# A planned kernel's sort keys and buffer numbers replaced: attention feeding a two-layer MLP, on one core

## The chip, the core and the metric

The kernel runs on one core of one Trainium2 chip. The metric is device time in microseconds (us) of one execution; lower is better. The engines of the core that matter here are TensorE (PE; its weight loads have rows of their own, PEld), VectorE (DVE), ScalarE (ACT), GpSimd (POOL, here only a queue that issues DMAs) and SyncE (SP, a queue that issues DMAs).

## What is computed

An attention over channels (2 batches, 6016 positions, 256 channels) gives 12032 tokens of 256 values, and these go through an MLP of 2048 hidden values with a slope of its own for each negative hidden value.

```python
qn = q / (norm(q, axis=1) + 1e-6);  kn = k / (norm(k, axis=1) + 1e-6)
s = kn.transpose(0, 2, 1) @ qn / tau          # 256 x 256 for each batch
a = softmax(s)
x = (v @ a).reshape(12032, 256)
h = x @ w_in                                  # 12032 x 2048
g = maximum(h, 0) + alpha * minimum(h, 0)
out = g @ w_out                               # 12032 x 256
```

## The kernel before

**Start.** The first 91 us read q and k of both batches, form the scores, fold the softmax into w_in (one matrix M for each batch) and convert the weights. This part is written out by hand and the change doesn't touch it.

**The planned part.** From then on the kernel works through 24 tiles of 500 or 504 tokens, and in each through 8 items, each of which makes 256 hidden values: 192 items, numbered i. Every product is made of three matmuls of fp32r halves (high by high, high by low, low by high; `passes`, L723), which is why matmuls come in threes on L725, L726 and L727. Three such matmuls are called one PE step below. Each item uses a fast scheme with seven products in place of eight:

- `pe(i, p)`, p = 0 to 6, L1227: one product each, into one half of one of two PSUM tiles: `a` (from the ring `ps_q`) or `b` (from `ps_r`). Each of the two tiles fills one PSUM bank and has two halves, `[:, 0]` and `[:, 1]`; each ring has two banks. pe6 writes a's half 1; pe0, pe5, pe4 and pe3 write or add to a's half 0; pe1 adds to b's half 0 and pe2 to b's half 1.
- `copy(i, 0)` on ACT, L1244 (called copy0): copies a's half 0 to b's half 0. `copy(i, 1)` on ACT, L1247 (copy1): copies a's half 1 to an SBUF tile `p7`, in the rows `p`.
- `add(i, 0)` and `add(i, 1)` on DVE, L1251 (add0, add1): a's half 0 plus `p7`, into b's half 1 (add0) or a's half 1 (add1).
- `act_n` on ACT and `dve_g` on DVE read the whole finished bank and make g.
- Then g is split into high and low halves. Most items (128) use a second fast scheme: `g_sums`, `x_high`, `x_low`, `t_high`, `t_low` and seven products `s2` into four PSUM banks X. The other 64 use `g_high`, `g_low` and four products `out_pe` with 500 columns. `t_low` is an ACT instruction of about 1 us and a DMA on POOL's queue that adds to its result.
- At a tile's end `combine_copy`, `combine` and `finish_out` empty the X banks and send the tile out. Parallel to all this v is loaded (POOL's queue) and split for the next tile (`v_sums`, `v_high`, `v_low`), and batch 1's norms and M are prepared (`load_T`, `square_T`, `m1_pe` and others).

**What an item's chain needs.** pe0, then copy0, then pe1 and pe5; pe6, then copy1; pe5 and copy1, then add0, then pe2 and pe4; pe4, then add1, then pe3; pe2 before act_n of b, pe3 before act_n of a; dve_g of a frees the bank of `a` for pe6 of item i+2.

**What sets the order.** `put` (L1598) gives each of the 5716 steps a sort key, the running sum of the numbers that the table `AT` (L45) holds under the step's name, in hundredths of a microsecond, and the list is sorted by key (L1731). Each engine and queue executes its own instructions in the order of this list; waits between engines are set by the framework from what each instruction reads and writes. The keys are no times of the chip. The table `SLOTS` (L564) names, for each tile that is taken from a ring (`Ring`, L625), the buffer that it gets.

Of the kernel before, what the change touches and what calls it, by code (L numbers as in the profile page):

```python
# [57 lines left out]
    ),  # L58
# [12 lines left out]
    ),  # L71
# [12 lines left out]
    ),  # L84
# [12 lines left out]
    ),  # L97
    "bcast1": (44517,),
    "combine0": (
        19167, 4002, 4060, 4010, 3823, 4201, 3733, 8365, 3789, 13160, 4381, 3982, 3733, 3733, 4181,  # L100
        4058, 4000, 4046, 3834, 2959
    ),
    "combine1": (
        19506, 3766, 4010, 4063, 3883, 4037, 3941, 8242, 4046, 12990, 4435, 3805, 3923, 3720, 4162,
        4121, 3844, 3996, 3813, 3019
    ),
    "combine2": (
        19797, 3714, 4032, 4075, 4158, 3627, 4217, 7952, 4169, 13197, 3982, 4189, 3799, 4160, 4192,
        3519, 3912, 4173, 3622, 2906
    ),  # L110
    "combine_copy": (
        18933, 4158, 3999, 3670, 4206, 4128, 3843, 7850, 4122, 13259, 4085, 4338, 3202, 4316, 4109,
        4010, 3886, 4258, 3215, 3318
    ),
    "conv_a": (9754, 698, 533),
    "conv_b": (9928, 452, 433, 267),
# [12 lines left out]
    ),  # L129
# [1635 lines left out]
```

## Time and profile before

| | us |
|---|---|
| median of 3 runs | 1172.31 (1170.83 to 1172.7) |
| profiled execution: its own time | 1170.25 |
| profiled execution: span from first to last instruction | 1168.5 |

| engine | busy us | share of the span | instructions |
|---|---|---|---|
| PE (matmuls) | 1123.1 | 96% | 8076 |
| PEld (weight loads) | 1042.6 | 89% | 8076 |
| DVE | 1002.6 | 86% | 1940 |
| ACT | 890.8 | 76% | 1578 |
| POOL | 176.2 | 15% | 214 |

The end of a matmul is modelled in this profile and matmuls overlap, so PE counts as busy for a while after the last one has been issued. The time by which a weight load was held is in the rows of PEld.

### The profile page before, as it was taken

The numbers are of one execution on the slowest core, as the hardware profiler recorded it, in microseconds if no ns is written. First come the engines' busy times: TensorE is split into PE (matmuls) and PEld (weight loads), VectorE is DVE, ScalarE is ACT, GpSimd is POOL, SyncE is SP. The second block draws the span as 40 slices with busy tenths as digits, with TensorE's granted clock in tenths as the row PEclk, the third lists the DMA queues.
The fourth block names the chain that finished last, engine by engine and source line by source line (L and its number), as shares of the span: only waits on it lengthen the run. The fifth ranks groups of instructions, "written<-read, shape, count | busy, mean of one in ns | idle before, by whom it ended". The sixth has DMA issues, their size and how long they took to land.

```text
span 1168.5 us, 21606 instructions
## 1 busy us (share of the span) xinstructions
PE 1123.1 (96%) x8076; PEld 1042.6 (89%) x8076; DVE 1002.6 (86%) x1940; ACT 890.8 (76%) x1578; POOL 176.2 (15%) x214
## 2 busy tenths in 40 slices
PE   9999999999989999999999999999999999999998
PEld 8888889988988898888989889899998999989998
DVE  6798999988887888888878988798998888888886
ACT  6786787878877787677766768688887778878785
POOL 0000011111111111011100011221222212221210
PEclk9999999999999999999999999999999999999999
DMA  9996244765664655143532126556667647756644
GB/s 340 358 330 231 73 112 112 168 150 124 147 158 101 155 122 121 36 95 81 128 88 54 54 68 128 127 114 134 145 133 141 129 98 141 155 129 124 130 91 88
DMA packets 70327, 158.20 MB, mean 135 GB/s; under 512 B 6800, under 2 KB 32496, under 8 KB 70096
## 3 DMA queue, kind: packets, MB, share of 16 engines
q0 software_dynamic: 38688, 93.92, 40.2%
q1 hardware_dynamic: 31536, 62.92, 15.5%
q8 instruction: 63, 1.03, 0.4%
q14 instruction: 40, 0.33, 0.1%
HBM read 59.78 MB, written 14.42 MB: 63 GB/s over the span
## 4 chain that ended last, share of the span: by engine, by line
PE 81%; ACT 8%; DVE 7%; issue 3%; DMA 1%; SPq 0%; ACTq 0%; DVEq 0%
PE X L725 11%; PE X L726 11%; PE X L727 11%; PE a L725 11%; PE a L727 8%; PE a L726 8%; PE S L1024 7%; PE b L725 4%; PE b L727 3%; PE b L726 3%; ACT g L1263 2%; DVE g L1271 2%; DVE b L1251 1%; PE pm L1176 1%; ACT p L1247 1%
## 5 line engine op out<-in xcount | busy, mean ns | idle before, releaser
L725 PE MATMUL a<-vs,m 128*128 128x250 f32 (+1 forms) x960 | 288.7, 301 | 32.9 <-ACT p L1247 10.4
L727 PE MATMUL a<-vs,m 128*128 128x250 f32 (+1 forms) x960 | 268.9, 280 | 0.0
L726 PE MATMUL a<-vs,m 128*128 128x250 f32 (+1 forms) x960 | 268.8, 280 | 0.0
L725 PEld LDWEIGHTS a<-vs,m 128*128 128x128 f32 x960 | 181.1, 189 | 69.4 <-ACT p L1247 18.9
L1370 POOL DMA_DIRECT2D tgl<-t x128 | 111.0, 867 | 665.9 <-ACT tgl L1369 452.3
L726 PEld LDWEIGHTS a<-vs,m 128*128 128x128 f32 x960 | 182.0, 190 | 2.9
L727 PEld LDWEIGHTS a<-vs,m 128*128 128x128 f32 x960 | 182.3, 190 | 0.0
L1271 DVE SCALAR_TENSOR_TENSOR g<-g,slope,a 128x500 f32<-128x500 f32 (+1 forms) x192 | 140.4, 731 | 25.7 <-ACT g L1263 24.4
L1263 ACT ACTIVATE g<-a 128x500 f32<-128x500 f32 (+1 forms) x192 | 113.5, 591 | 59.1 <-PE a L727 50.3
L1369 ACT ACTIVATE tgl<-t 128x1000 fp32r<-128x1000 f32 (+1 forms) x128 | 133.9, 1046 | 15.1 <-DVE t L1349 8.6
L1271 DVE SCALAR_TENSOR_TENSOR g<-g,slope,b 128x500 f32<-128x500 f32 (+1 forms) x192 | 139.9, 730 | 6.2 <-ACT g L1263 5.5
L1251 DVE TENSOR_TENSOR b<-a,p 128x250 f32<-128x250 f32 (+1 forms) x192 | 81.4, 424 | 66.4 <-PE b L727 27.5
L1376 ACT CAST tgh<-t 128x1000 fp32r<-128x1000 f32 (+1 forms) x128 | 131.7, 1032 | 0.2 <-DVE t L1349 0.2
L1263 ACT ACTIVATE g<-b 128x500 f32<-128x500 f32 (+1 forms) x192 | 113.2, 590 | 20.4 <-PE b L727 16.7
L1359 DVE TENSOR_TENSOR xl<-g,xh 128x750 fp32r<-128x750 f32 (+1 forms) x128 | 119.6, 934 | 6.2 <-ACT xh L1354 6.0
L1247 ACT COPY p<-a 128x250 f32<-128x250 f32 (+1 forms) x192 | 70.8, 369 | 63.5 <-PE a L727 63.0
L725 PE MATMUL b<-vs,m 128*128 128x250 f32 (+1 forms) x384 | 110.6, 288 | 4.8 <-DVE b L1251 4.6
L1354 ACT CAST xh<-g 128x750 fp32r<-128x750 f32 (+1 forms) x128 | 105.3, 823 | 12.1 <-PE X L726 8.9
L725 PE MATMUL X<-tgh,ws 128*128 128x250 f32 (+1 forms) x384 | 107.5, 280 | 1.7 <-ACT c L1427 1.5
L1349 DVE TENSOR_TENSOR t<-g,t 128x250 f32<-128x250 f32 (+1 forms) x256 | 105.9, 414 | 2.9
L726 PE MATMUL b<-vs,m 128*128 128x250 f32 (+1 forms) x384 | 107.5, 280 | 0.0
L727 PE MATMUL b<-vs,m 128*128 128x250 f32 (+1 forms) x384 | 107.5, 280 | 0.0
(140 smaller groups left out, 2990.7 us busy)
## 6 DMA issues: line engine op xcount, KB each, us to landing
tgl<-t POOLq DMA_DIRECT2D x91, 500.0 KB, 4.5
tgl<-t POOLq DMA_DIRECT2D x37, 504.0 KB, 4.6
kqT<-kqT_dram SPq DMA_DIRECT2D x20, 512.0 KB, 4.2
kq<-k_dram SPq DMA_DIRECT2D x39, 256.0 KB, 5.6
kq<-q_dram SPq DMA_DIRECT2D x39, 256.0 KB, 5.6
v<-vT_dram POOLq DMA_DIRECT2D x16, 500.0 KB, 5.0
vs<-vt POOLq DMA_DIRECT2D x32, 250.0 KB, 4.9
outT_dram<-c SPq DMA_DIRECT2D x30, 250.0 KB, 2.8
```

The costliest lines, as they stand in the source:

```text
L725: nc.tensor.matmul(out, wh, xh, start=first, stop=False, **s)
L726: nc.tensor.matmul(out, wh, xl, start=False, stop=False, **s)
L727: nc.tensor.matmul(out, wl, xh, start=False, stop=last, **s)
L1251: nc.vector.tensor_tensor(out=h_t[i][n][:, 1, :h], in0=h_t[i][1][:, 0, :h], in1=p7_t[i][:, :h], op=ALU.add)
L1263: nc.scalar.activation(blocks(g_t[i], i, 2 * fi, 2 * fi + 2), h_t[i][fi][:, :, : half_of(i)], AF.Relu, scale=-1.0)
L1271: nc.vector.scalar_tensor_tensor(out=g, in0=g, scalar=slope[:, f : f + 1], in1=h_t[i][fi][:, :, : half_of(i)], op0=ALU.mult, op1=ALU.add,)
L1349: nc.vector.tensor_tensor(out=o, in0=x, in1=y, op=ALU.subtract)
L1354: nc.scalar.copy(xs_t[i][0][:, h : 4 * h], g_t[i][:, h : 4 * h])
L1359: nc.vector.tensor_tensor(out=xs_t[i][1][:, h : 4 * h], in0=g_t[i][:, h : 4 * h], in1=f32(xs_t[i][0][:, h : 4 * h]), op=ALU.subtract,)
L1369: nc.scalar.activation(ts[1][:, :w], tt_t[i][:, :w], AF.Copy, scale=-1.0)
L1370: nc.gpsimd.dma_start(out=ts[1][:, :w], in_=tt_t[i][:, :w], accum_op=ALU.add)
L1376: nc.scalar.copy(ts[0][:, :w], tt_t[i][:, :w])
```

## The change

Only numbers change. All keys in `AT` are new, and of `SLOTS` the strings of the rings gh, gl, raw and rn (the rings of `a`, `b`, p7 and the split v keep theirs). The set of steps, every instruction, all shapes and all DMAs stay as they are. The keys are said to come from a search that counts each wait on a PSUM tile for the whole bank.

```diff
@@ AT @@
     "act_n0": (
-        10450, 710, 501, 334, 661, 243, 586, 115, 962, 805, 144, 626, 104, 640, 689, 528, 191, 563, 575,
+        10382, 200, 905, 673, 346, 421, 345, 940, 314, 523, 497, 686, 191, 622, 415, 841, 3, 559, 825,
...
-    "keep_wi": (9983,),
-    "load_T0": (11798, 4093, 4192, 4281, 3916, 4079, 4425, 3156),
+    "keep_wi": (13308,),
+    "load_T0": (12995, 3046, 4590, 3855, 4320, 4223, 3444, 3708),
...
@@ SLOTS @@
     gh=(
-        "012012012012120120120120120121021021012012012102120102102012012012012102102102102102102102"
+        "012012012012012012012012012010210120210210210120120120120120120121201021021020120120120121"
...
```

What this makes of the order can be counted in the two sorted lists, with no run. "PE work between" is the work that the list puts on PE between the end of one step and the start of the other, taking 0.35 us for a step of three matmuls with 250 columns and 0.69 us for one with 500; under 0.9 us means two such steps or fewer.

| in the sorted list | before | after |
|---|---|---|
| items whose copy1 stands ahead of pe0 | 27 | 7 |
| of these, under 0.9 us of PE work between pe6 and pe0 | 16 | 0 |
| items whose add0 stands ahead of pe1, with under 0.9 us between pe5 and pe1 | 14 | 0 |
| items whose pe1 stands ahead of add0 | 61 | 36 |
| of these, under 0.9 us between pe1 and the first of pe2 and pe4 | 24 | 1 |
| under 0.9 us between pe0 and pe5 | 28 | 2 |
| under 0.9 us between pe5 and pe4 | 21 | 0 |
| under 0.9 us between pe4 and pe3 | 41 | 0 |
| under 0.9 us between pe5 and pe2 | 5 | 0 |
| under 0.9 us between pe0 and pe1 | 3 | 1 |
| under 1.9 us between pe3 of item i and pe6 of item i+2 | 22 | 30 |
| t_low with under 2 us between the last product that reads its buffer and itself | 46 | 71 |
| copy0 and copy1 with under 2 us between the last reader of their buffer and themselves | 88 | 118 |
| tiles whose first use of v has a key less than 10 us behind the step that frees v's buffer | 0 | 7 |

`keep_wi`, a DMA on SP's queue, stood ahead of the first `load_T` there and stands behind it now.

## Rows read from the trace of the kernel before

**Rows 1.** The page: span, busy time of engines, chain that ended last by engine.

```profile
span 1168.5 us, 21606 instructions
...
PE 1123.1 (96%) x8076; PEld 1042.6 (89%) x8076; DVE 1002.6 (86%) x1940; ACT 890.8 (76%) x1578; POOL 176.2 (15%) x214
...
PE 81%; ACT 8%; DVE 7%; issue 3%; DMA 1%; SPq 0%; ACTq 0%; DVEq 0%
```

**Rows 2.** Groups by line, PEld: busy us, mean ns, then idle before, releasers.

```profile
L727 PEld LDWEIGHTS a<-vs,m 128*128 128x128 f32 x960 | 182.3, 190 | 0.0
...
L725 PEld LDWEIGHTS a<-vs,m 128*128 128x128 f32 x960 | 181.1, 189 | 69.4 <-ACT p L1247 18.9 <-DVE b L1251 16.2 <-ACT b L1244 10.2
...
L725 PEld LDWEIGHTS b<-vs,m 128*128 128x128 f32 x384 | 72.7, 189 | 11.3 <-DVE b L1251 8.4 <-ACT b L1244 0.4
```

**Rows 3.** Waits of PEld: who waited for whom, us, times, longest.

```profile
PEld a L725 <- ACT p L1247: 18.9, 35, 1.6
PEld a L725 <- DVE b L1251: 16.2, 32, 1.1
PEld a L725 <- ACT b L1244: 10.2, 23, 2.0
PEld b L725 <- DVE b L1251: 8.4, 17, 1.2
PEld a L725 <- DVE a L1251: 5.7, 14, 1.1
...
PEld a L725 <- DVE g L1271: 4.2, 12, 0.8
```

**Rows 4.** Timeline, 347.4 to 351.2 us: start, duration, engine, line, [idle before <-releaser].

```profile
348.36 0.27 PE L725 MATMUL a<-vs,m 128*128 128x250 f32 x1
...
348.82 0.28 PE L726 MATMUL a<-vs,m 128*128 128x250 f32 x1
...
348.94 0.28 PE L727 MATMUL a<-vs,m 128*128 128x250 f32 x1
...
350.15 0.37 ACT L1247 COPY p<-a 128x250 f32<-128x250 f32 x1
...
350.58 0.38 PE L725 MATMUL a<-vs,m 128*128 128x250 f32 x1 [1.35 <-ACT p L1247]
...
350.80 0.28 PE L726 MATMUL a<-vs,m 128*128 128x250 f32 x1
```

**Rows 5.** Groups by line, DVE and ACT: the costs of add0 and copy0.

```profile
L1251 DVE TENSOR_TENSOR b<-a,p 128x250 f32<-128x250 f32 (+1 forms) x192 | 81.4, 424 | 66.4 <-PE b L727 27.5 <-PE a L727 18.0 <-ACT p L1247 11.6
...
L1244 ACT COPY b<-a 128x250 f32<-128x250 f32 (+1 forms) x192 | 70.3, 366 | 46.8 <-PE a L727 38.7 <-DVE g L1271 6.7 <-DVE a L1251 0.4
```

**Rows 6.** Waits of all engines: two of ACT for a buffer.

```profile
ACT b L1244 <- DVE g L1271: 6.7, 9, 1.1
...
ACT tgl L1369 <- PE X L726: 5.1, 9, 1.0
```

**Rows 7.** Stretches of 3.4 us: PE, PEld, DVE, ACT, POOL busy, PEclk, DMA.

```profile
531.30:534.70 3.40, 1.90 (x14) 1.50 (x13) 3.03 (x7) 1.39 (x3) 0.00 (x0) 1.00 0.00 0
534.80:538.20 3.40, 3.40 (x16) 3.27 (x15) 2.80 (x6) 2.76 (x5) 0.87 (x1) 0.50 0.00 0
...
746.40:749.80 3.40, 1.51 (x11) 1.11 (x10) 2.38 (x5) 0.64 (x1) 1.08 (x1) 1.00 1.00 164
749.80:753.20 3.40, 3.27 (x15) 3.30 (x16) 2.60 (x6) 1.97 (x4) 1.61 (x2) 0.50 0.85 142
```

**Rows 8.** The line that loads v (L916): its DMAs' time to landing.

```profile
DMA to landing us min/median/max: 3.9/5.1/7.8
```

**Rows 9.** DMA issues: keep_wi, count, size, median us to landing.

```profile
wi_kept<-wi SPq DMA_DIRECT2D x1, 2048.0 KB, 11.1
```

More of the change, by code (lines that the diff above doesn't have):

```diff
@@ L46 @@
     "act_n0": (
[11 rows of a table removed]
[11 rows of a table added]
     ),
     "act_n1": (
[11 rows of a table removed]
[11 rows of a table added]
     ),
     "add0": (
[11 rows of a table removed]
[11 rows of a table added]
     ),
     "add1": (
[11 rows of a table removed]
[11 rows of a table added]
     ),
-    "bcast1": (44517,),
+    "bcast1": (43553,),
     "combine0": (
-        19167, 4002, 4060, 4010, 3823, 4201, 3733, 8365, 3789, 13160, 4381, 3982, 3733, 3733, 4181,
-        4058, 4000, 4046, 3834, 2959
+        19305, 4057, 4208, 4016, 3542, 4137, 3965, 8487, 3837, 13327, 3588, 4234, 3954, 4007, 3681,
+        4091, 4202, 3682, 4016, 3030
     ),
     "combine1": (
-        19506, 3766, 4010, 4063, 3883, 4037, 3941, 8242, 4046, 12990, 4435, 3805, 3923, 3720, 4162,
-        4121, 3844, 3996, 3813, 3019
+        19682, 3863, 4041, 4222, 3613, 4021, 3859, 8451, 3910, 13350, 3738, 4120, 4032, 3878, 3703,
+        4094, 4127, 3869, 3808, 3138
@@ L106 @@
     ),
     "combine2": (
-        19797, 3714, 4032, 4075, 4158, 3627, 4217, 7952, 4169, 13197, 3982, 4189, 3799, 4160, 4192,
-        3519, 3912, 4173, 3622, 2906
+        19769, 4048, 4005, 4050, 3908, 3893, 3776, 8546, 3845, 13441, 3482, 4296, 4159, 4276, 3404,
+        3891, 3985, 4182, 3681, 2905
     ),
     "combine_copy": (
-        18933, 4158, 3999, 3670, 4206, 4128, 3843, 7850, 4122, 13259, 4085, 4338, 3202, 4316, 4109,
-        4010, 3886, 4258, 3215, 3318
-    ),
-    "conv_a": (9754, 698, 533),
@@ L116 @@
-    "conv_b": (9928, 452, 433, 267),
+        19137, 3827, 4364, 4014, 3699, 4223, 3374, 8350, 4531, 13134, 3378, 4404, 4185, 3499, 3725,
+        4065, 3719, 4626, 4024, 2862
+    ),
+    "conv_a": (9888, 493, 840),
+    "conv_b": (9822, 297, 396, 1145),
     "copy0": (
[11 rows of a table removed]
[11 rows of a table added]
     ),
     "copy1": (
[11 rows of a table removed]
[11 rows of a table added]
     ),
     "dve_g0": (
[11 rows of a table removed]
[11 rows of a table added]
     ),
     "dve_g1": (
[11 rows of a table removed]
-    ),
-    "evac": (14616,),
-    "exps": (46058, 159),
-    "finish_last0_0": (107633,),
-    "finish_last0_1": (107817,),
-    "finish_last1_0": (107712,),
@@ L174 @@
-    "finish_last1_1": (107642,),
[11 rows of a table added]
+    ),
+    "evac": (12926,),
+    "exps": (46754, -46),
+    "finish_last0_0": (107611,),
+    "finish_last0_1": (107856,),
+    "finish_last1_0": (107751,),
+    "finish_last1_1": (107799,),
     "finish_out0": (
-        15366, 4207, 3726, 4054, 3994, 4226, 3898, 3872, 4374, 3801, 4154, 4940, 4205, 3784, 4391, 3960,
-        3989, 3984, 3776, 4034, 3852, 4036, 3772
+        15433, 4253, 3989, 4088, 4047, 3924, 3800, 4109, 4066, 4045, 4355, 5014, 4065, 4057, 4003, 3751,
+        4005, 3983, 3762, 3948, 4219, 3853, 3777
@@ L178 @@
     ),
     "finish_out1": (
-        15247, 4572, 3830, 4030, 4109, 4032, 3827, 3974, 4549, 4080, 3749, 4818, 4812, 3732, 3880, 3997,
-        4157, 3992, 4083, 3540, 4051, 4146, 3633
+        15706, 4143, 4250, 3832, 3986, 4304, 3454, 3833, 4897, 3911, 3939, 4408, 4815, 3929, 4028, 4153,
+        4117, 3980, 3787, 3974, 4084, 3948, 3741
     ),
     "g_high0": (
[4 rows of a table removed]
[4 rows of a table added]
     ),
     "g_high1": (
[4 rows of a table removed]
[4 rows of a table added]
     ),
     "g_low0": (
[4 rows of a table removed]
[4 rows of a table added]
     ),
     "g_low1": (
[4 rows of a table removed]
[4 rows of a table added]
     ),
     "g_sums0": (
[7 rows of a table removed]
[7 rows of a table added]
     ),
     "g_sums1": (
[7 rows of a table removed]
[7 rows of a table added]
     ),
@@ L225 @@
     "g_sums2": (
[7 rows of a table removed]
-    ),
-    "keep_wi": (9983,),
[60 rows of a table removed]
-    "norms": (43377,),
[2 rows of a table removed]
[7 rows of a table added]
+    ),
+    "keep_wi": (13308,),
[60 rows of a table added]
+    "norms": (42546,),
[2 rows of a table added]
     "out_pe0_0": (
[4 rows of a table removed]
[4 rows of a table added]
     ),
     "out_pe0_1": (
[4 rows of a table removed]
[4 rows of a table added]
     ),
     "out_pe1_0": (
[4 rows of a table removed]
[4 rows of a table added]
     ),
     "out_pe1_1": (
[4 rows of a table removed]
[4 rows of a table added]
     ),
     "pe0": (
[11 rows of a table removed]
[11 rows of a table added]
     ),
     "pe1": (
[11 rows of a table removed]
[11 rows of a table added]
     ),
     "pe2": (
[11 rows of a table removed]
[11 rows of a table added]
     ),
     "pe3": (
[11 rows of a table removed]
[11 rows of a table added]
     ),
     "pe4": (
[11 rows of a table removed]
[11 rows of a table added]
     ),
     "pe5": (
[11 rows of a table removed]
[11 rows of a table added]
     ),
     "pe6": (
[11 rows of a table removed]
-    ),
-    "pe_fill": (9725, 77, 1009, -679, 429, -112, -155),
-    "reload_wi": (54149, 764, 584, 688, 2138, 563, 669, 461),
[11 rows of a table added]
+    ),
@@ L415 @@
+    "pe_fill": (9825, 1, 294, 205, 207, 189, 262),
+    "reload_wi": (55378, 373, 895, 966, 517, 612, 860, 409),
     "s20": (
[7 rows of a table removed]
[7 rows of a table added]
     ),
     "s21": (
[7 rows of a table removed]
[7 rows of a table added]
     ),
     "s22": (
[7 rows of a table removed]
[7 rows of a table added]
     ),
     "s23": (
[7 rows of a table removed]
[7 rows of a table added]
     ),
     "s24": (
[7 rows of a table removed]
[7 rows of a table added]
     ),
     "s25": (
[7 rows of a table removed]
[7 rows of a table added]
     ),
     "s26": (
[7 rows of a table removed]
-    ),
[5 rows of a table removed]
-    "s_weights_high": (13815, 917, 398, 269, 1259, 274, 47936),
-    "s_weights_low": (14257, 777, 440, 36, 1183, 442, 47966),
-    "scores": (44840, 729),
-    "split_eT": (47200, 341),
-    "split_wi_h": (54593, 568, 582, 832, 1971, 367, 839, 635),
@@ L488 @@
-    "split_wi_l": (54660, 766, 697, 1745, 957, 250, 833, 979),
-    "split_wo": (9957, 176, 573, 731, 277),
[3 rows of a table removed]
-    "sums_T": (42339,),
-    "t_high": (
[7 rows of a table removed]
[7 rows of a table added]
+    ),
[5 rows of a table added]
+    "s_weights_high": (14004, 246, 920, 915, 881, 1615, 45576),
+    "s_weights_low": (14284, 560, 639, 714, 1156, 1505, 46268),
+    "scores": (44315, -343),
+    "split_eT": (47158, 170),
+    "split_wi_h": (55420, 685, 959, 684, 871, 195, 789, 1732),
+    "split_wi_l": (55518, 987, 725, 758, 751, 507, 474, 1751),
+    "split_wo": (9836, 544, 440, 130, 996),
[3 rows of a table added]
@@ L502 @@
+    "sums_T": (42386,),
+    "t_high": (
[7 rows of a table added]
     ),
     "t_low": (
[7 rows of a table removed]
-    ),
-    "transposes1": (46447,),
-    "v_add": (65958, 3724, 4045, 4753, 3757, 2898, 5216, 3773, 3009, 5173),
[7 rows of a table added]
+    ),
+    "transposes1": (47008,),
+    "v_add": (64610, 5454, 4467, 3026, 4542, 4312, 3151, 3885, 4818, 2836),
     "v_high0": (
-        11993, 2864, 3914, 5231, 3673, 4230, 2622, 4320, 3801, 5140, 3164, 5449, 3409, 4458, 4919, 3383,
-        3819, 4020, 3537, 4928, 3906, 3177, 3936
+        12017, 2749, 5291, 3548, 4524, 2315, 6649, 1709, 4648, 4328, 3789, 5380, 2118, 4742, 3717, 5216,
+        3545, 4651, 3460, 3983, 4847, 3691, 2666
@@ L517 @@
     ),
     "v_high1": (
-        12576, 3352, 3581, 3761, 4555, 4813, 3664, 3939, 5082, 3406, 4184, 5105, 2952, 2846, 5166, 3587,
-        3685, 3714, 4401, 3077, 5007, 4135, 4514
+        13018, 2659, 4090, 5031, 2614, 4392, 4173, 4205, 2544, 6597, 1455, 7038, 3411, 3277, 3443, 4792,
+        3698, 3535, 5452, 2781, 3739, 3846, 3734
     ),
     "v_high2": (
-        12662, 3882, 3841, 4740, 3294, 4049, 2996, 3882, 4793, 4136, 2831, 4727, 5615, 3445, 3944, 3802,
-        3951, 3817, 3897, 3849, 5155, 3448, 3303
+        12960, 2637, 4084, 3959, 3638, 4192, 4011, 3780, 5350, 4207, 3550, 3586, 3770, 4746, 4953, 3230,
@@ L525 @@
+        4041, 4243, 3184, 3874, 3879, 4526, 3611
     ),
     "v_low0": (
-        12383, 3998, 4599, 3382, 4231, 3599, 2505, 6556, 3017, 4460, 3137, 5784, 4389, 2829, 4997, 2808,
-        4187, 3669, 4157, 4993, 4016, 2311, 6543
+        12052, 4474, 4195, 4304, 4462, 4091, 3687, 3352, 4144, 3714, 5092, 3903, 3792, 3626, 3306, 5674,
+        4446, 4427, 4134, 1747, 5590, 2846, 4963
     ),
     "v_low1": (
-        13616, 3739, 4476, 3484, 4118, 4269, 4131, 4097, 3770, 3972, 3722, 5103, 4516
+        13551, 2229, 5541, 4603, 2833, 4473, 3551, 4949, 2882, 5381, 3371, 4763, 4323
@@ L532 @@
     ),
     "v_low2": (
-        13285, 4337, 2836, 4668, 4068, 4141, 3592, 4324, 3961, 3628, 4213, 4905, 4391
+        13024, 4398, 3652, 4169, 3166, 4560, 4577, 3871, 3596, 4307, 3189, 3787, 5742
     ),
-    "v_minus": (65876, 3626, 3173, 4075, 3895, 4200, 3719, 5457, 3041, 4428),
+    "v_minus": (64573, 5378, 4296, 3047, 4303, 4697, 2709, 3432, 4483, 3538),
     "v_sums0": (
-        11344, 2914, 4030, 3958, 3758, 4688, 3237, 3939, 4605, 3694, 4280, 4433, 4440, 3805, 3843, 4510,
-        4167, 3625, 3919, 3878, 4052, 3805, 3070
+        11220, 2710, 4383, 3884, 3809, 4217, 4220, 3523, 4227, 3537, 4388, 5298, 3200, 4187, 3602, 4392,
+        5005, 3844, 4019, 3860, 3299, 4660, 3553
@@ L540 @@
     ),
     "v_sums1": (
-        11994, 2321, 4538, 4029, 3264, 4644, 3562, 3937, 4464, 5279, 2722, 4220, 5322, 2968, 4518, 3801,
-        4545, 3597, 3844, 3640, 4641, 3667, 3861
+        11373, 3257, 3741, 4288, 3413, 4484, 3889, 4254, 3904, 3369, 4277, 5624, 2750, 5257, 3858, 3484,
+        4853, 3674, 4046, 3815, 3760, 4179, 3661
     ),
     "x_high": (
[7 rows of a table removed]
[7 rows of a table added]
     ),
     "x_low": (
[7 rows of a table removed]
[7 rows of a table added]
     ),
@@ L565 @@
     gh=(
-        "012012012012120120120120120121021021012012012102120102102012012012012102102102102102102102"
-        "101021021021021021021021021021021021021021021021021021021020120120120120120210210212012012"
-        "012012012102102101201201"
-    ),
-    gl=(
-        "012012012012012012012010210210201201201021021021020120120120120210210212012102102102102102"
-        "120120120120120120120120120120120210210212012012021021021021021020120120120120120120120120"
+        "012012012012012012012012012010210120210210210120120120120120120121201021021020120120120121"
+        "021201210212012012012012012012012010210210201201201021021020120120201201201201201201201201"
+        "210210210210210202102102"
+    ),
+    gl=(
+        "012012012012012012012010210210201202101201201201201201201202102021021020120120120120210201"
+        "201201201201201201201201202102102102102102102102102102102102102102102102120120120120120120"
         "1201201201201201201201"
@@ L590 @@
     raw=(
-        "012301230123012301230123012332012310320123103201231032012310320123103201231032010312302103"
-        "123021031230210312302103123021031230210312310320132013201320123103201231032012310320123103"
-        "201231032012310320123103201231032012310320123103201231032012310320123103201231032010312302"
-        "10312302103123021031230210312"
-    ),
-    rn=(
-        "012301230123012301230123012301230123012301230132013023102301230123021320310213021301230123"
-        "012301230132102310231032103210321032102310231023102310231023102310231023102310213021320132"
-        "031230132102301203120312302103120312031021320312012301321023102302103123021031203102132031"
-        "023102301230132103201302310213203103201321023012301230210321031203120310213023120321302103"
-        "1"
+        "012301230123012301230123012332023201231032012310323120130231201302012310320123103201232031"
+        "021320310213203102132031021320310213203102013201301303130130231201302312013023120130231201"
+        "302312013023120130231201302312013023130120321301203213012032130120321303201231032010312302"
+        "10312303102132031021320310213"
+    ),
+    rn=(
+        "012301230123012301230123012301230123012301230123102132013201320312031203121031203210321021"
+        "302312013210213201302130213021320132013201320130231023102031201321032102310231023012103210"
+        "231023120132031320130213023120132013210230123102312013021320310213021301203210320132012301"
+        "320123021302103123013201320123103210321301203213012310321032013201320132031023103210231023"
+        "0"
     ),
```

726 rows, old and new, of the table AT are left out of this document.

## The prediction

> **What bounds the kernel now.** I read the page first: busy times, then the chain that ended last [rows 1]. PE's matmuls are busy for 96% of the span and PE makes up 81% of the chain; 15% of it, some 175 us, lie on ACT and DVE. So PE carries the kernel, and the question is how long it is held. Matmul busy time hides most of that, because a matmul's end is modelled 0.28 us behind its start while the next may start 0.12 us behind it (348.82 and 348.94 in [rows 4]): a hold of up to 0.16 us leaves no idle time at all. The weight loads show it better. For the followers (L727) they were never held; for the first matmul of a PE step (L725) they were held for 69.4 us on tile a and 11.3 us on tile b, together 80.7 us [rows 2]. A restart costs something more: after the wait at 350.58 the second matmul came 0.22 us later, not 0.12 [rows 4], 0.10 us for each of the 133 waits of [rows 3], 13 us. PE's loss is therefore near 94 us, and a kernel that never held PE would span near 1075 us. Nothing in the edit changes what PE has to do, so all that it can give lies in these 94 us.
>
> The Trainium skill's page "Perfetto Trace Analysis" (Identifying the Most-Contended Engine) says that matmul busy time is a poor measure of the headroom and that weight-load busy time is a better one. By the first the headroom here would be 45 us, by the second 126 us; the 94 us counted from the waits lie between.
>
> Then I read who held the weight loads [rows 3], and in one wait of the timeline what kind it was [rows 4]. There pe6 of an item has written half 1 of bank a at 348.36, and pe0 of the same item, which writes half 0, starts only at 350.58, when copy1 (350.15 to 350.52), which reads half 1, has ended. The two halves have nothing to do with each other: the wait is for the whole bank. Every row "a <- ACT p" is of this kind, since copy1 reads half 1 alone and pe0, pe5, pe4 and pe3 touch half 0 alone.
>
> **The change part by part.** Steps only move; no instruction, wait rule or DMA comes or goes. I go by kinds of wait; each costs its row plus 0.10 us for each time.
>
> (1) Whole-bank waits. "a <- ACT p" is 18.9 us in 35 waits, with restarts 22.4. "b <- DVE b" is 8.4 us in 17, with restarts 10.1; it is either pe1 behind add0, which touch different halves, or pe2 behind add0, which share one. The table has 14 tight places of the first kind and 5 of the second, so I put 14/19 of it, 7.4, here: 29.8 us together [rows 3]. In the new list the tight places of both kinds are gone (16 to 0, 14 to 0), and pe0 to pe5 falls from 28 to 2. Copies that are late for another reason will still hold some. I take 4 us as left and 26 as gained, with 15 (half stays) and 30 as bounds. DVE, too, loses a whole-bank wait: add0, which writes b's half 1, stood 27.5 us waiting for pe1, which writes b's half 0 [rows 5], with g's work queued behind it. Its tight places go from 24 to 1. I count no gain of its own for that; it is why (2) should not stay.
>
> (2) True waits. "a <- DVE b" (pe4 behind add0), "a <- ACT b" (pe5 behind copy0) and "a <- DVE a" (pe3 behind add1) are 16.2, 10.2 and 5.7 us in 32, 23 and 14 waits, 32.1 us in 69; with restarts 39.0 [rows 3]. What a step through DVE needs: 0.16 us until the matmul before it has ended, 0.424 us for the add [rows 5], and 0.06 us until PE starts (350.52 to 350.58 in [rows 4]); with as much for the add's own start, 0.70 us. Two PE steps of 0.35 us give exactly that, so any lateness of ACT or DVE holds PE; three leave 0.35 us of slack. The table's five counts under 0.9 us fall from 98 places to 3. The mean wait is 32.1/69 = 0.47 us. If each of the 69 became 0.35 us shorter, that is 24 us; but some stood at looser places already, where nothing is promised. I take six in ten of it, 15 us. Bounds: 8, if two in three waits stand elsewhere, and 29, if three in four of the 39.0 go because DVE and ACT are no longer blocked.
>
> (3) What is given back. pe6 behind dve_g of item i-2 has more tight places, 22 to 30; its row is 4.2 us in 12, 5.4 with restarts [rows 3], so +2.0 us (0 to 4). ACT reuses buffers sooner behind their readers: t_low 46 to 71, copies 88 to 118. Its rows for such waits are 5.1 and 6.7 us [rows 6]; in proportion they grow by 0.54 x 5.1 + 0.34 x 6.7 = 5.0 us of ACT's time. Behind a held t_low or copy0 on ACT stand copies and act_n, for which PE and DVE wait; ACT has 277.7 us of idle time [rows 1], so I let 3 of the 5 reach PE (0 to 8, the upper end with both rows grown by two thirds and none of it absorbed). v's first use comes as close as 6.5 us behind the freeing of its buffer; the load lands 5.1 us after its issue, 7.8 at worst [rows 8], so the seven places hold DVE (v_sums, with add and dve_g queued behind it) now and then by about 1 us: 1 us in all (0 to 4). keep_wi now issues behind the first load_T on SP, which waits for a buffer that the last of the early matmuls of batch 1's scores frees (key 110 us). It lands 11.1 us later [rows 9], and s_weights_high, the first to overwrite what it reads, has a key of 140 us. That cover hides it: 0, and 11 us once if it were gone. The other moved loads and stores on SP and POOL have more room than their time to landing: 0. Together 6 us (0 to 16).
>
> (4) The clock. Two stretches of 3.4 us ran at half the clock (0.50, the lower level), each right behind a stretch in which PE was busy for 1.90 and 1.51 of 3.40 us; each cost 1.7 us [rows 7]. A denser PE could lose them or meet others: +1 us (0 to 3.4).
>
> Sum: 26 + 15 - 6 + 1 = 36 us off. The profiled execution took 1170.25 us, its span 1168.5, with 1.75 us around it that stay; it would take 1134. The median of the runs is 2 us above it, so the forecast for the median is 1172.31 - 36 = **1136 us**.
>
> **The rivals.** *The stall moves along.* PE arrives earlier at places where the same ACT and DVE instructions are late, DVE being 86% busy [rows 1]. For it: DVE would have to do its 1002.6 us within 1132. Against it: three steps between. It leaves (1) minus what comes back, half of 26, and (2) at nothing, less 3 or so: gain 8 to 13, 1159 to 1164 us. Chance 0.12.
>
> *ACT held at its buffers: slower.* If the tight reuse is real at every place, 71 t_low wait 5.1/9 = 0.57 us, 40 us, and a quarter of the 118 copies wait 6.7/9 = 0.74 us, 22 us [rows 6]; ACT's queue is in order, and copy0, copy1 and act_n stand behind. From 42 us of it on that reach PE (the 36 and the 6 already counted), the kernel is slower; with 50 to 60 it ends at 1180 to 1190. For it: the counts went up by half. Against it: ACT's idle time, and the row of now shows only 9 waits for 46 tight places. Chance 0.07.
>
> *No order helps.* Tiles a and b have two banks each, and a wait for a bank that dve_g must free would return wherever the step is put; then the rest is 1170 to 1174 us. The row against it: such waits are 4.2 us of the 69.4 [rows 3]. Chance 0.05. This is what "Perfetto Trace Analysis" (Optimization Strategy) in the Trainium skill says of a gap that repeats: it can mean too little PSUM for the next tile.
>
> *More.* DVE and ACT, no longer blocked, are on time nearly everywhere: 30 + 29 + 3 - 0 is the most, 62 us; 1110 to 1117 us. Chance 0.08.
>
> That the change doesn't do what it says is out: the counts are of the lists themselves.
>
> **How the numbers follow.** The forecast (gain 10 to 55 us about 36) has 0.68. Its bounds run from 15 + 8 - 12 = 11 us to 55, so 1117 to 1161. The range leaves out the slower case, the unchanged one, and most of the tails of the two others: 1116 to 1163 us. Faster by over 0.2% (2.3 us, about what a measurement here can tell from none): 0.68 + 0.12 + 0.08 = 0.88; within: 0.05; slower: 0.07.
>
> **What would show it.** Held weight loads on a and b (80.7 us) near 45 us; "a <- ACT p" under 5 us and add0's wait for pe1 under 8; "a <- DVE b" and "a <- ACT b" at about 16 together; "a <- DVE g" at 5 to 7. The stall that moves would show as the same 70 to 80 us under other names, DVE's above all; ACT held at its buffers as "tgl <- PE X" and "b <- DVE g" of tens of us. The prediction is wrong if PE's loss stays above 75 us or falls below 30.

## The result and the profile after

The changed kernel takes 1096.0 us (median of 4 runs, 1093.9 to 1096.8) against 1171.6 for the kernel before on the same chip: ratio 0.935, 95% interval 0.934 to 0.937. The gain is 75 us; 36 were forecast, with 10 to 55 as the range. The direction was right, the size was not.

The page of after, as [rows 1]: span, busy times, the chain that ended last.

```profile
span 1092.1 us, 21567 instructions
...
PE 1081.0 (99%) x8076; PEld 1031.3 (94%) x8076; DVE 995.1 (91%) x1940; ACT 890.5 (82%) x1578; POOL 175.9 (16%) x214
...
PE 87%; DMA 5%; DVE 4%; issue 2%; ACT 2%; POOL 0%; ACTq 0%; POOLq 0%; DVEq 0%; SPq 0%
```

Weight loads are busy for nearly as long as before (1042.6 us then, 1031.3 now), in a span that is 76.4 us shorter. How long they were held, as [rows 2], and who held them, as [rows 3]:

```profile
L725 PEld LDWEIGHTS a<-vs,m 128*128 128x128 f32 x960 | 180.9, 188 | 16.9 <-DVE g L1271 4.5 <-ACT p L1247 1.9 <-DVE a L1251 1.7
...
L725 PEld LDWEIGHTS b<-vs,m 128*128 128x128 f32 x384 | 72.4, 189 | 2.6 <-ACT b L1244 0.7
```

```profile
PEld a L725 <- DVE g L1271: 4.5, 9, 1.2
PEld a L725 <- ACT p L1247: 1.9, 2, 1.7
PEld a L725 <- DVE a L1251: 1.7, 3, 1.2
...
PEld a L725 <- DVE b L1251: 1.2, 3, 0.8
...
PEld b L725 <- ACT b L1244: 0.7, 1, 0.7
...
PEld a L725 <- ACT b L1244: 0.2, 1, 0.2
```

The hold on a and b fell from 80.7 to 19.5 us, 61.2 us. Waits for ACT and DVE there fell from 134 (the 133 of [rows 3] and one more) to 19, which at 0.10 us for a restart is 11.5 us. The granted clock is 1.000 over the span instead of 0.997: the two half-clock stretches of [rows 7] are not there, 3.5 us. Together 76.2 us of the 76.4. So nearly the whole gain is PE standing less, and the ledger of the prediction holds; what it put into the ledger was too small.

On the other side of those waits, DVE's add0 and ACT's two copies, as [rows 5] (busy, mean ns, idle before, releasers):

```profile
L1251 DVE TENSOR_TENSOR b<-a,p 128x250 f32<-128x250 f32 (+1 forms) x192 | 81.3, 424 | 20.5 <-PE a L727 9.8 <-ACT p L1247 4.9 <-PE b L727 2.7
...
L1247 ACT COPY p<-a 128x250 f32<-128x250 f32 (+1 forms) x192 | 71.2, 371 | 19.7 <-PE a L727 18.7
L1244 ACT COPY b<-a 128x250 f32<-128x250 f32 (+1 forms) x192 | 70.7, 368 | 29.3 <-PE a L727 23.4 <-DVE g L1271 3.9 <-DVE a L1251 0.7
```

The line of copy1 in the kernel before:

```profile
L1247 ACT COPY p<-a 128x250 f32<-128x250 f32 (+1 forms) x192 | 70.8, 369 | 63.5 <-PE a L727 63.0
```

The adds and copies last as long as before. add0's whole-bank wait for pe1 fell from 27.5 to 2.7 us [rows 5], and its wait for copy1 from 11.6 to 4.9. The largest wait of this kind is copy1's own: it needs pe6 alone, yet it stood 63.0 us waiting for PE. Taking each copy1 by its place in the sorted list and by the end of its pe6 in the trace, pe6 had already ended in some 52 of these 63.0 us: copy1 stood behind pe5 (58 items) or pe0 (107), which write the other half of the bank. In the changed kernel the row is 18.7 us, some 14 of it of this kind. ACT and DVE being on time, which the sum gave no gain of its own, is a large part of what changed.

### The profile page after: what moved, and what is told of

Read it like the earlier page. It is cut to its first block, busy times and chain, and to the rows that moved or that the text cites. A ratio compares the mean times of both kernels' runs of the same rounds, so it can differ in the third digit from the quotient of the medians.

```text
span 1092.1 us, 21567 instructions
## 1 busy us (share of the span) xinstructions
PE 1081.0 (99%) x8076; PEld 1031.3 (94%) x8076; DVE 995.1 (91%) x1940; ACT 890.5 (82%) x1578; POOL 175.9 (16%) x214
## 4 chain that ended last, share of the span: by engine, by line
PE 87%; DMA 5%; DVE 4%; issue 2%; ACT 2%; POOL 0%; ACTq 0%; POOLq 0%; DVEq 0%; SPq 0%
PE X L726 13%; PE X L725 13%; PE X L727 13%; PE a L725 9%; PE a L726 9%; PE a L727 9%; PE S L1024 8%; PE b L725 4%; PE b L727 4%; PE b L726 4%; DMA tgl<-t 3%; PE pm L1176 1%; DVE g L1271 1%; DVE t L1349 1%; DMA kqT<-kqT_dram 1%
## 5 line engine op out<-in xcount | busy, mean ns | idle before, releaser
L725 PE MATMUL a<-vs,m 128*128 128x250 f32 (+1 forms) x960 | 272.5, 284 | 5.5 <-DVE g L1271 2.1
L726 PE MATMUL a<-vs,m 128*128 128x250 f32 (+1 forms) x960 | 268.3, 279 | 0.2 <-DMA vs<-vt 0.2
L727 PE MATMUL a<-vs,m 128*128 128x250 f32 (+1 forms) x960 | 268.3, 279 | 0.0
L1370 POOL DMA_DIRECT2D tgl<-t x128 | 110.8, 866 | 591.4 <-ACT tgl L1369 403.9
L725 PEld LDWEIGHTS a<-vs,m 128*128 128x128 f32 x960 | 180.9, 188 | 16.9 <-DVE g L1271 4.5
L726 PE MATMUL X<-tgl,ws 128*128 128x250 f32 (+1 forms) x384 | 107.2, 279 | 0.5 <-DMA tgl<-t 0.3
L725 PE MATMUL b<-vs,m 128*128 128x250 f32 (+1 forms) x384 | 107.3, 280 | 0.2 <-ACT b L1244 0.2
L727 PE MATMUL b<-vs,m 128*128 128x250 f32 (+1 forms) x384 | 107.2, 279 | 0.0
L726 PE MATMUL b<-vs,m 128*128 128x250 f32 (+1 forms) x384 | 107.2, 279 | 0.0
L725 PE MATMUL X<-tgh,ws 128*128 128x250 f32 (+1 forms) x384 | 107.1, 279 | 0.0
L727 PE MATMUL X<-tgh,ws 128*128 128x250 f32 (+1 forms) x384 | 107.0, 279 | 0.0
```

Of the source, the lines that this page charges most:

```text
L725: nc.tensor.matmul(out, wh, xh, start=first, stop=False, **s)
L726: nc.tensor.matmul(out, wh, xl, start=False, stop=False, **s)
L727: nc.tensor.matmul(out, wl, xh, start=False, stop=last, **s)
L1370: nc.gpsimd.dma_start(out=ts[1][:, :w], in_=tt_t[i][:, :w], accum_op=ALU.add)
```

## The experiments

Three theories stood against each other at first. K (knock-on): whole-bank waits make ACT and DVE late, and that lateness makes the true waits. S (slack): two-step distances make the true waits by themselves. B: the order on ACT and DVE and the rings' buffers count. A fourth, F (fit), came out of the first four runs. "True waits" are those of steps that touch the same half of a bank, as in (2) of the prediction, "whole-bank waits" those of steps that touch different halves, as in (1). "True rows" below are the waits of PEld on a for DVE b, ACT b and DVE a together: 32.1 us before [rows 3], 3.1 us after. Where a list was redone "by readiness", the order came from playing the lists through with the durations of the traces; the diffs show the sorted list of steps, item in brackets, since the keys themselves say nothing; steps that lie between are left out of them. The runs were made on several chips, each beside the kernel before, which took 1168.6 to 1170.7 us there (1171.6 beside the changed kernel); where runs of different chips are compared below, some 3 us are open.

### Places mended by their distance: b_bank, b_wide, b_both, a_tight

```diff
 b_bank                 b_wide                a_tight (PE's steps)
  pe6(43)                out_pe0_0(96)         s22(26)
 +pe0(43)               +pe2(100)             +pe3(30)
  copy1(43)              pe4(100)              s20(26)
 -pe0(43)               -pe2(100)             -pe3(30)
                         pe1(100)              pe6(31)
                        -pe3(100)
                         pe6(101)
                         out_pe0_1(97)
                        +pe3(100)
```

b_both mends both kinds, but some 25 of the tight places stay.

> The kernel before with the whole-bank places alone mended: pe0 put directly behind pe6 of its item in the 27 items where copy1 stood ahead of it, and pe1 put behind add0, one microsecond or more after pe5, in 33 items. Buffers and the orders of ACT, DVE, POOL and SP stay as before; the tight true distances stay too (pe0>pe5 26, pe5>pe4 32, pe4>pe3 36 places under 0.9 us). Theory K (knock-on: the whole-bank waits hold ACT's and DVE's queues, and their lateness makes the true waits): most of the 75 us come off, 1100 to 1112 us; a<-DVE b and a<-ACT b together fall from 26 to under 8 us. Theory S (slack: the two-step distances make the true waits by themselves): only the bank rows go, 25 to 30 us off, 1142 to 1148 us; a<-DVE b and a<-ACT b stay at 20 us or more. Theory B (buffers and ACT/DVE order are what counts): under 15 us off, 1157 or more.

> The kernel before with the true distances alone widened: pe5, pe4, pe3 put one step or more later wherever they stood under 0.9 us behind the step before them in the chain of their item (98 places down to 6). Every whole-bank order stays as before (copy1 ahead of pe0 in 27 items, pe1 ahead of add0 in 61), buffers and the other engines' orders too. Theory K: the lateness stays, 5 to 20 us off, 1152 to 1167 us, a<-ACT p and b<-DVE b still 20 us or more together. Theory S: the true waits go, 35 to 50 us off, 1122 to 1137 us, a<-DVE b and a<-ACT b under 6 us together. Theory B: under 15 us off.

> The kernel before with both mended (whole-bank places as in the first kernel, true distances widened, 98 places to about 25), buffers and the orders of ACT, DVE, POOL and SP as before. Theories K and S alike: within 15 us of the changed kernel, 1096 to 1111 us. Theory B: 1125 us or more, because the buffers and the order on ACT and DVE are still the old ones.

> The changed kernel with the two-step distances put back: pe5, pe4, pe3 pulled earlier in the items where the kernel before had them under 0.9 us behind the step before (pe0>pe5 29, pe5>pe4 19, pe4>pe3 36, 86 places instead of 3); whole-bank orders, buffers and the other engines' orders stay as in the changed kernel. Theory K: under 12 us slower than the changed kernel, 1096 to 1108 us, since ACT and DVE stay on time. Theory S: 30 to 45 us slower, 1126 to 1141 us, with a<-DVE b and a<-ACT b back at 20 us or more. Theory B: under 12 us slower as well.

Measured: b_bank 1152.4 us (ratio to the kernel before 0.986, 0.983 to 0.988); b_wide 1171.6 (1.002, 1.001 to 1.003); b_both 1153.1 (0.987, 0.984 to 0.990); a_tight 1136.6 (0.972, 0.970 to 0.974). The waits of PEld in b_wide and in a_tight, then one of ACT in b_bank:

```profile
PEld a L725 <- ACT p L1247: 19.5, 31, 1.8
PEld a L725 <- DVE b L1251: 12.5, 26, 0.8
...
PEld a L725 <- DVE g L1271: 7.6, 17, 0.9
PEld a L725 <- ACT b L1244: 7.3, 21, 1.2
```

```profile
PEld a L725 <- DVE a L1251: 17.0, 26, 1.7
PEld a L725 <- ACT b L1244: 9.6, 17, 2.1
PEld a L725 <- DVE b L1251: 6.2, 12, 1.8
PEld a L725 <- ACT p L1247: 5.3, 11, 1.4
```

```profile
ACT p L1247 <- PE a L727: 66.9, 89, 2.3
```

Widening nearly all of the 98 two-step places gave nothing in the old lists: the true rows fell only from 32.1 to 23.4 us, and what they lost, other rows (DVE g, ACT b on tile b) took; by the sorted list the widening also makes other places tight (pe3 to pe6 of item i+2: some 30 places instead of 22). Narrowing them again in the new lists costs 41 us, and the true rows are back at 32.8. The bank places alone gave 17 us, and both together no more than that. No theory passes all four: K wanted at least 60 us from b_bank, S at least 35 from b_wide, and B under 12 of loss from a_tight. But b_bank is no full test of K: it leaves copy1 against pe5 as it was, and by putting pe0 ahead of copy1 it frees PE and makes copy1 wait, so that ACT's largest whole-bank wait did not fall but rose, from 63.0 to 66.9 us (65.1 in b_both). Distances were worth 41 us in one set of lists and nothing in the other; on what that depends these runs don't show by themselves. This led to F: what holds PE is in-order lists that are out of step in play, an engine standing at one step while the next one has its input.

### Who waits for whom, and PE's order by readiness: b_dirs, a_dirs_back, b_pe, b_dirs_pe

```diff
 b_dirs                 a_dirs_back           b_pe (PE's steps)
  copy0(50)              pe6(42)               s24(25)
 +copy1(50)             +copy1(42)            +s25(25)
  pe5(50)                pe0(42)               pe5(29)
 -copy1(50)             -copy1(42)            -s25(25)
                                              +pe1(29)
                                               pe6(30)
                                              -pe1(29)
```

In the first two no engine's own order changes: copy1 is on ACT, pe5 and pe0 are on PE, and only their order against each other is turned, which decides who waits for the bank. b_dirs_pe does both, by the same two rules worked out anew: 21 pairs on a and b stand otherwise than in b_dirs, and some 400 of PE's 2512 positions otherwise than in b_pe.

> The kernel before with every engine's own order untouched (PE, ACT, DVE, POOL, SP) and the same buffer for every tile. Only for 86 pairs of steps on two engines that touch different halves of one PSUM bank it is turned round which of the two waits for the other (30 times copy1 now ahead of pe5, 20 times add0 ahead of pe1, 11 times copy1 ahead of pe0, 8 times the other way, and so on), by which of them has its input first. The 98 tight true distances stay. Theory F (fit: what holds PE is lists that are out of step in play, each in-order engine standing at a step whose partner is not there yet while the next one is ready): 25 to 40 us off, 1130 to 1145 us, with a<-ACT p under 8 us and the true rows lower too, since ACT and DVE are late less often. Theory S (static distance): at most the bank rows, 25 us, and the true rows a<-DVE b, a<-ACT b, a<-DVE a stay at 28 us or more together. Theory B (the order on ACT and DVE and the buffers): as the first kernel with the bank places mended, under 20 us off, 1150 or more.

> The kernel before with PE's steps alone re-ordered: wherever the step that comes next has no input yet and one of the two behind it has, that one goes first (some 400 positions changed). Orders of ACT, DVE, POOL and SP, buffers, and who waits for whom at every PSUM bank stay as before. The counts of tight true distances stay as well: pe0>pe5 29, pe5>pe4 19, pe4>pe3 43 under 0.9 us, copy1 ahead of pe0 in 27 items and pe1 ahead of add0 in 61. Theory F: 25 to 40 us off, 1130 to 1145 us. Theory S: the counts have not changed, so under 10 us off, 1160 or more. Theory B: under 15 us off.

> The kernel before with both: bank pairs turned by readiness (94 pairs) and PE's steps taken by readiness among three (some 400 positions). ACT, DVE, POOL, SP orders and buffers as before; 77 of the 98 tight true distances are still there (pe5>pe4 19, pe4>pe3 39). Theory F: 45 to 60 us off, 1110 to 1125 us, the rest up to the changed kernel being the order on ACT and DVE. Theory S: 77 of 98 tight places left, so at most 35 us off, 1135 or more. Theory B: 1140 us or more.

> The changed kernel with every engine's own order and every buffer untouched; only 40 pairs of steps on two halves of one PSUM bank are turned against readiness (copy1 now ahead of pe0 23 times, copy1 ahead of pe5 12 times, add0 ahead of pe1 5 times), the 40 closest ones. True distances stay wide (3 of 98 tight places). Theory F: 18 to 32 us slower than the changed kernel, 1114 to 1128 us; a<-ACT p and b<-DVE b carry it (over 12 us together). If whole-bank waits were cheap to turn (lists with this much slack absorb them): under 8 us slower, 1104 or less.

Measured: b_dirs 1139.3 us (0.974, 0.972 to 0.976), b_pe 1143.7 (0.977, 0.975 to 0.979), b_dirs_pe 1128.5 (0.964, 0.962 to 0.967), a_dirs_back 1124.1 (0.961, 0.959 to 0.963). F named three of the four ranges; b_dirs_pe came out 3.5 us above its range. The waits of ACT, PEld and DVE in b_dirs:

```profile
ACT p L1247 <- PE a L727: 25.4, 50, 2.1
...
PEld a L725 <- ACT p L1247: 12.6, 38, 1.1
PEld b L725 <- DVE b L1251: 11.4, 26, 1.0
...
PEld a L725 <- ACT b L1244: 7.6, 13, 2.2
...
DVE b L1251 <- PE b L727: 5.6, 11, 0.9
DVE b L1251 <- ACT p L1247: 5.0, 8, 1.9
...
PEld a L725 <- DVE b L1251: 4.4, 13, 0.6
...
PEld a L725 <- DVE a L1251: 2.7, 9, 0.7
```

This run shows where a good part of the true waits comes from. Every distance between PE's steps, every order and every buffer is the old one, and turning 86 pairs takes copy1's wait for PE from 63.0 to 25.4 us, add0's wait for pe1 from 27.5 to 5.6 and for copy1 from 11.6 to 5.0, and the true rows from 32.1 to 14.7. PE's order is the same in both traces, so they can be compared step by step. In the 70 items in which a pair on a or b was turned the true rows fell from 20.0 to 3.3 us, in the other 122 only from 12.2 to 11.4: the lateness comes from the item's own copy or add. Not all of it is gone. In nine items pe4's wait for add0 (6.0 us together) has become pe1's wait for the same add0 (3.9 us), which is booked in the whole-bank row "b <- DVE b". So some 13 of the 32.1 us of true waits, four tenths, were lateness handed on from whole-bank waits. PE's own two whole-bank rows together fell by little, from 27.3 to 24.0 us (18.9 and 8.4 before, 12.6 and 11.4 here; "under 8" for the first was a miss): the largest part of the gain of 31 us is in rows that are called true. b_pe shows that it is not the bank alone: with all pairs left as they were, and with as many tight true places as before, PE's order by readiness gives 27 us. Both rules together give 42, not 58, so they mend in part the same waits.

In a_dirs_back 40 pairs turned the wrong way cost 28 us, 0.7 us each, and almost all of it is in one row:

```profile
PEld a L725 <- ACT p L1247: 28.4, 35, 1.8
...
PEld a L725 <- DVE a L1251: 1.4, 2, 1.2
...
PEld a L725 <- DVE b L1251: 1.2, 3, 0.8
```

Here the true rows stay down (2.6 us). That is no test of whether wide distances absorb lateness: with copy1 ahead it is PE that is held, and copy1's own wait for PE fell, from 18.7 to 12.3 us.

### More of the same: a_pe, b_all, a_all

```diff
 a_pe (PE's steps)      b_all (DVE's steps)   a_all (ACT's steps)
  pe1(48)                g_sums1(54)           copy0(68)
 +pe2(48)               -add1(55)              copy1(68)
  pe3(48)                g_sums2(54)          +act_n0(67)
 -pe2(48)                v_low1(7)             act_n1(67)
                        -add0(56)             -act_n0(67)
                        +add1(55)
```

> The changed kernel with the same re-ordering on top: PE's steps by readiness among three (53 positions differ), 17 bank pairs turned by readiness. Theory F: the changed kernel's lists fit nearly everywhere, so little is left: 1 to 5 us under it, 1091 to 1095 us, with a<-DVE g (4.5 us) lower. Theories S and B: no difference, 1095 to 1097 us.

> The kernel before with the orders of PE, ACT and DVE all three redone by readiness from its own order (among the next six steps of PE and five of ACT and DVE the one whose input is there first, with 0.02 us of margin on every ACT and DVE step so that a small lateness does not turn it round); 180 PSUM pairs turned. SP's and POOL's orders as before, and every tile keeps the physical buffer that it has in the kernel before. Tight true distances fall by themselves to about 30 of 98. Theory F: the lists fit, 1092 to 1108 us, next to the changed kernel. Theory B in its form 'buffers': 1115 us or more, since the buffers are the old ones.

> The changed kernel with the orders of PE, ACT and DVE redone in the same way (readiness, with margin), buffers as in it; 96 PSUM pairs turned. Theory F: its lists fit nearly everywhere and PE has little left to lose (the weight loads' waits on a and b are 19.5 us), so 0 to 8 us under it, 1088 to 1096 us. Theory B: no gain, 1095 to 1100 us.

Measured: a_pe 1099.5 us (0.939, 0.938 to 0.941), b_all 1145.0 (0.979, 0.975 to 0.983), a_all 1124.1 (0.961, 0.959 to 0.963). All three missed what F had named. a_pe, with 53 positions moved and 17 pairs turned, is 3.5 us slower than the changed kernel, which had little left to gain. b_all and a_all end 49 and 28 us above it, and a few long stalls carry much of that. ACT's waits for the loads of k and q in b_all, PEld's longest wait there, and a stretch of a_all with two stalls of 4.7 and 4.1 us (us, then busy PE, PEld, DVE, ACT, POOL, granted clock, DMA):

```profile
ACT kqT L1042 <- DMA kqT<-kqT_dram: 20.6, 9, 9.3
...
PEld a L725 <- DVE a L1251: 13.1, 8, 9.4
```

```profile
300.00:500.00 200.00, 188.06 (x1383) 177.87 (x1382) 168.25 (x334) 150.98 (x281) 28.25 (x35) 0.97 0.50 116
```

The play-through knew nothing of when those loads land, so in the new lists ACT stands in front of them (20.6 us; the kernel before 4.5, the changed kernel 3.9), and everything behind it on ACT stands too, once for 9.3 us. With this stall the clock fell: in b_all the granted clock was 0.50 from 346.7 to 357.0 us, while PE stood and for 3.7 us after it had gone on; over the span it is 0.989. These two runs therefore say nothing on the buffers, for which b_all was meant; they show that readiness has to count loads as well.

### The buffers alone: a_buf, bdp_buf

```diff
 SLOTS, ring rn, first numbers, a_buf
-01230123012301230123012301230123012301230123012310213
+01230123012301230123012301230123001230123012301230123
```

bdp_buf does the same to b_dirs_pe. (The strings are cut; 79 and 88 of 361 tiles come to follow another tile.)

> The changed kernel with every engine's order and every PSUM pair as in it; only the buffers of the ring of g and t tiles (and a few of gl) are picked anew by a plain rule, the one that comes free first: 79 of the 361 tiles of that ring follow another tile than in the changed kernel. If the buffers searched for are a part of the gain: 8 us or more slower, 1104 or more. If they are not (theory F: order and bank pairs are the whole): within 4 us, 1092 to 1100 us.

> The kernel before with its bank pairs turned and PE re-ordered (1128.5 us), and now its buffers picked anew by the plain rule: 88 of 361 tiles of the ring of g and t follow another tile, a few of gh and gl. Orders of all engines as in that kernel. In its trace ACT waits 10.9 us in 10 waits for a g buffer that DVE or a DMA still reads. If these hold the 32 us that are left: 8 us or more faster, 1120 or less, with those rows under 4 us. If the buffers are not what is left: within 4 us, 1124 to 1133 us.

Measured: a_buf 1105.4 us (0.946, 0.945 to 0.948), 9.4 us above the changed kernel; bdp_buf 1138.2 (0.975, 0.973 to 0.977), 9.7 above b_dirs_pe; by the ratios both are some 13 us. In the first, one wait carries most of it. ACT's waits for a g buffer that a DMA still reads (3.0 us in the changed kernel), the time to landing of these DMAs (L1370), and the stretches around the longest wait:

```profile
ACT g L1263 <- DMA tgl<-t: 12.5, 6, 7.3
...
DMA to landing us min/median/max: 4.3/4.6/10.0
```

```profile
658.40:661.80 3.40, 3.40 (x29) 3.27 (x28) 2.66 (x6) 0.64 (x2) 0.00 (x0) 1.00 0.98 172
661.80:665.20 3.40, 0.49 (x5) 0.28 (x3) 0.00 (x0) 0.00 (x0) 0.00 (x0) 1.00 0.86 215
665.20:668.60 3.40, 0.37 (x2) 0.40 (x3) 1.02 (x2) 1.88 (x4) 0.00 (x0) 0.51 0.04 10
668.60:672.00 3.40, 3.40 (x18) 3.40 (x18) 2.23 (x4) 1.88 (x4) 0.85 (x1) 0.50 0.33 103
672.00:675.40 3.40, 3.40 (x30) 3.40 (x30) 1.89 (x5) 2.19 (x5) 0.00 (x0) 0.99 0.66 129
```

ACT and DVE stand still for a whole stretch, PE with them, and the next two run at half the clock. The DMA it stands for is the slowest of its kind, 10.0 us from issue to landing against 4.6 in the median. The same DMA took 9.8 us in the changed kernel, where ACT has no wait of that length (1.5 us is the longest for these DMAs). So the buffers do count: one ill-chosen buffer out of hundreds costs about as much as 20 waits of the mean 0.47 us. In bdp_buf the same row is 15.9 us in 14 waits, against 5.4 in 6 in b_dirs_pe. The plain rule was worse than both searched strings, so neither run says how much of the last 32 us, from b_dirs_pe to the changed kernel, the buffers hold. That b_dirs_pe keeps buffers chosen for another order shows in its trace (5.5 and 5.4 us; 0.7 and 3.0 in the changed kernel):

```profile
ACT g L1263 <- DVE gl L1287: 5.5, 4, 1.7
ACT g L1263 <- DMA tgl<-t: 5.4, 6, 2.3
```

How the 32 us divide between ACT's and DVE's orders, the loads and the buffers stays open. Moving one engine's new order into the old kernel alone was not tried.

### One ledger for all

Span, held weight loads on a and b (L725), waits for ACT and DVE there, and granted clock, each from its trace; the rest is span minus held, minus 0.10 us for each wait, minus (1 - clock) x span.

| kernel | span | held | waits | clock | rest |
|---|---|---|---|---|---|
| before | 1168.5 | 80.7 | 134 | 0.997 | 1071 |
| after | 1092.1 | 19.5 | 19 | 1.000 | 1071 |
| b_bank | 1151.8 | 64.9 | 124 | 0.997 | 1071 |
| b_wide | 1169.7 | 82.1 | 130 | 1.000 | 1075 |
| b_both | 1150.7 | 64.9 | 110 | 1.000 | 1075 |
| b_dirs | 1136.1 | 53.2 | 106 | 1.000 | 1072 |
| b_pe | 1142.2 | 56.6 | 98 | 0.999 | 1075 |
| b_dirs_pe | 1124.4 | 41.5 | 63 | 1.000 | 1077 |
| b_all | 1145.7 | 50.8 | 49 | 0.989 | 1077 |
| a_tight | 1134.6 | 58.2 | 81 | 0.998 | 1066 |
| a_dirs_back | 1121.7 | 46.4 | 52 | 0.998 | 1068 |
| a_pe | 1096.9 | 20.3 | 20 | 0.998 | 1072 |
| a_all | 1122.1 | 37.5 | 40 | 0.994 | 1074 |
| a_buf | 1103.3 | 30.2 | 28 | 0.996 | 1066 |
| bdp_buf | 1136.9 | 49.5 | 70 | 0.998 | 1078 |

Where a stall and a stretch at the lower clock overlap, the terms for the hold and for the clock count the same time twice. In b_all, a_buf and a_all PE worked for only 16.4, 3.9 and 9.5 us at the lower clock. Half of that is 8.2, 1.9 and 4.7 us, not the 12.6, 4.4 and 6.7 that the column gives, and their rests are then 1082, 1068 and 1076. So the ledger closes to within some 16 us. The 0.10 us for a restart comes from one wait [rows 4].

## Why the prediction was wrong in size

**The frame held.** PE carries the kernel, and its floor is near 1075 us: the rest of the ledger is 1066 to 1082 in all fifteen kernels. The Trainium skill's "Perfetto Trace Analysis" (Identifying the Most-Contended Engine) says to judge TensorE's headroom by the share of peak arithmetic and by weight-load busy time, and not by matmul busy time. The trace agrees on the last: by matmul busy time 45 us were to be had, and 76 came.

In the terms of the prediction the 76.2 us are 30.4 (1), 35.2 (2), 0 (3), 3.5 (4) and 7.1 in rows that had no term, against 26 + 15 - 6 + 1 = 36. Half of the 40 us that it lacked are in (2).

**(1) Whole-bank waits: right.** 26 of 29.8 us were forecast as gained, for PE's own waits. "a <- ACT p" with restarts fell from 22.4 to 2.1, and "b <- DVE b" from 10.1, of which 7.4 were counted here, to none that the list of waits shows.

**(2) True waits: the step that failed.** It priced them by the distance between PE's steps: 24 us if each of 69 became 0.35 us shorter, six in ten of that because "some stood at looser places already, where nothing is promised". With restarts they fell from 39.0 to 3.8 us, 35 instead of 15, and beyond the upper bound of 29. Two things were wrong. Waits of (2) depend not on the distance alone: b_dirs lowers their rows by 17.4 us without touching a distance, some 13 of them lateness of a copy or add that had stood in a whole-bank wait. The prediction saw a part of this lateness (add0's 27.5 us, "it is why (2) should not stay") and let it into the upper bound and "More" only, with no term in the sum; the larger part, copy1's 63.0 us of waiting for PE, it did not name. And no one price fits a distance: widening was worth nothing in the old lists (b_wide), narrowing cost 41 us in the new ones (a_tight). How the 35 us divide between lateness and distance stays open.

**(3) Given back: 6 us forecast, nothing found.** "a <- DVE g" went from 4.2 us in 12 waits to 4.5 in 9; ACT's two waits for buffers, 5.1 and 6.7 us [rows 6], fell to 4.3 and 3.9 although their tight places rose from 46 to 71 and from 88 to 118:

```profile
ACT tgl L1369 <- PE X L726: 4.3, 11, 1.1
...
ACT b L1244 <- DVE g L1271: 3.9, 10, 0.9
```

A count of tight places said nothing here. That the danger is real is shown by a_buf, not by the changed kernel.

**(4) The clock: 1 us forecast as gained, 3.5 gained** between the two profiled executions. Which execution was profiled has a part in it: the granted clock of the kernel before is 0.995 to 1.000 in the executions on record, that of the changed kernel 0.998 to 1.000. Nor is it shown that fewer holds are the cause: b_wide, with 82.1 us of them, has 1.000.

**What the sum left out.** Besides the six rows of [rows 3] (63.6 us before, 9.5 after), weight loads on a and b were held for 17.1 us in smaller rows, now 10.0: 7 us that no term had.

**The rivals.** "More" named the right mechanism, DVE and ACT on time nearly everywhere, but stopped at 62 us because it took the bound of 29 for (2) and had nothing for the smaller rows. "The stall moves along" did not happen in the changed kernel; b_wide, where the hold stayed at 82.1 us, came near it. "No order helps" is out; the Trainium skill's "Perfetto Trace Analysis" (Optimization Strategy) says that a repeating gap can mean too little PSUM, and here the gaps went with the same PSUM and another order. Of the signs, a<-ACT p under 5 us (1.9) and add0's wait under 8 us (2.7) came true; held loads near 45 (19.5), true rows for DVE b and ACT b near 16 (1.4) and "a <- DVE g" at 5 to 7 (4.5) did not, and PE's loss, 19.5 + 1.9 us, is below the 30 at which the prediction called itself wrong.

## What to carry to other kernels

In lists that several in-order engines work through together, a wait can have its cause upstream (four tenths of the true waits here): before pricing waits one by one, look at the waits of the partner engines too, ask how late the partner is and what it stood at before, and don't add the price of "partner late" to that of "too little room" as if they were independent. A wait that only guards a shared bank can be turned round without moving any engine's work (31 us here from 86 pairs), so look at it first, and at both sides of it: a turn that frees PE can make ACT late (b_bank). Count held weight loads, restarts and the granted clock into one ledger; when its rest stays nearly the same from kernel to kernel, as here within some 16 us, what a change can still give is read from the holds.

## What the hardware showed that was not expected

A long stall of PE was paid for beyond its own length. In a_buf PE worked 0.49 and 0.37 us of two stretches of 3.40 us; the granted clock was 0.51 in the second and 0.50 in the next one, in which PE was busy throughout, and 0.99 after it. PEld's longest wait on tile a is 6.1 us. In the second stretch PE hardly worked, so the lower clock cost it little there; in the next one it took half of 3.40 us, 1.7. The two together, 7.8, are most of the 9.4 by which the kernel is slower.
